# Attention with a key and value cache: every score product as a pair of 64-row tiles, the third dimension block crossing to the other bank, and new instruction lists

## The chip, the cores and the metric

The kernel runs on one core of one Trainium2 chip. The core has a matrix engine (TensorE, in the profile PE for its matmuls and PEld for its weight loads), VectorE (DVE), ScalarE (ACT), GpSimd (POOL) and SyncE (SP), which here only issues transfers. Each engine works through its own list of instructions; engines wait for each other through semaphores. The metric is the time of one execution on the device in microseconds, the median of several runs. The profile is of one execution.

## The reference: what is computed

```python
B, Sq, D = 8, 112, 640
H, Sk, Dh = 32, 512, 192
q = (x @ wq).reshape(B, Sq, H, Dh).transpose(0, 2, 1, 3)
scores = einsum("bhqd,bhkd->bhqk", q, k_cache) * Dh ** -0.5
p = softmax(scores, axis=-1)
o = einsum("bhqk,bhkd->bhqd", p, v_cache)
return o.transpose(0, 2, 1, 3).reshape(B, Sq, H * Dh) @ wo
```

All inputs are bf16. Eight batches, 32 heads, 112 query rows, 512 keys and a head size of 192, which is one and a half times the 128 rows of the matrix array. That odd size is what the change is about.

## The kernel before

The heads are taken in four rounds of eight. A *step* `n` (64 of them) is one batch and four heads of a round (`place`, L74); a *group* `g` (eight of them) is a round and half of the batches. For each group, `q_fill` (L584) projects the queries of two heads at a time: a pair of heads has 384 dimensions, so three blocks `c` of 128 dimensions, each five matmuls that write a PSUM bank, which `evQ` on ScalarE copies to the SBUF tile `qr`. For each step, in order of its own data:

- `qc` (L608, VectorE) copies `qr` to the tile `qh` with the two halves of 64 partitions exchanged, so that either half of a dimension block is to be had in either half of the partitions.
- `scores` (L618, TensorE) multiplies queries by keys. The keys stand transposed in `kt`. A column of `kt` holds two neighbouring keys, an even and an odd one, whose 2 x 192 dimensions lie one after another over three blocks of 128 rows: block 0 and the first half of block 1 belong to the even key, the second half of block 1 and block 2 to the odd one. A head has 256 such columns. Scores of even keys go to the even bank of a pair `j` of heads (banks 0 and 2), those of odd keys to the odd bank (1 and 3), 256 columns a head. A step has 8 matmuls over 128 rows (`Sm`, L635 and L637: block 0 to the even bank, block 2 to the odd one) and then 8 over 64 rows (`St`, L648 and L650: the halves of block 1, as four pairs that use the upper and the lower half of the array).
- `softmax` (L655): `smax` (VectorE, L663) scales and finds the maximum from PSUM, `exp` (ScalarE, L668), `rc` and `norm` (VectorE, L680 and L672).
- `transposes` (L694) turn the probabilities on TensorE in pairs of 64 and 48 rows (`PT`, L706); `evPT` (L719) copies them out. Five late steps are turned by a transfer instead (`TD`, L690).
- `values` (L722) multiply by the values: `PVt` (L739) in tiles of 64 columns, then `PVm` (L750) in full ones; `evPV` (ScalarE, L760) writes `oT_sb`.
- Per group, `o_half` (L767, L772) multiplies by `wo`, and `oacc` (VectorE) adds over the rounds. `OF` and `oout` turn and store the result.

The keys of the first seven pairs of head sets and batches are transposed on TensorE (`KT`, L561, copied by `evK`, L572); the others come transposed by the transfer itself (L139).

The order of all this is written out by hand: `ORDER_PE`, `ORDER_ACT`, `ORDER_DVE` and `ORDER_SP` list the operations of each engine. `Plan.run` (L35) goes through an engine's list, and before each operation waits for those that it depends on, with a semaphore count per engine. Row-tiled operations count on two semaphores, `PE` and `PE2`, one for each half of the array. A PSUM bank passes from one user to the next by a dependency on the copy that emptied it (`fill`, L896). Three layouts of the array occur: 128 rows by 128 columns (`Q`, `O`, `PVm`, `Sm`), 64 rows (`St`, `PT`, `KT`) and 128 by 64 (`PVt`).

The matmuls of one step's scores, before:

```python
e.matmul(ps[0:SQ, 2 * j, hs], ev, ktb[:, :, 0, cs(i)], start=(h == 0), stop=False, ...)           # Sm, even bank
mm = e.matmul(ps[0:SQ, 2 * j + 1, hs], od, ktb[:, :, 2, cs(i)], start=(h == 0), stop=False, ...)  # Sm, odd bank
m1 = e.matmul(ps[0:SQ, 2 * j, hs], ev, ktb[0:64, :, 1, cs(i)], start=False, stop=True, ...)       # St, rows 0 to 63
m2 = e.matmul(ps[0:SQ, 2 * j + 1, hs], od, ktb[64:128, :, 1, cs(i)], start=False, stop=True, ...) # St, rows 64 to 127
```

Of the kernel before, what the change touches and what calls it, by code (L numbers as in the profile page):

```python
# [11 lines left out]
class Plan:  # L12

# [6 lines left out]
    def add(self, eng, name, deps, emit, sem=None, inc=1):  # L20
        assert name not in self.ops, name
        self.ops[name] = dict(eng=eng, deps=deps, emit=emit, sem=sem or eng, inc=inc)

    def number(self):
        self.count = {}
        for eng, names in self.order.items():
            for n in names:
                o = self.ops[n]
                o["at"] = {}
                for s in o["sem"] if isinstance(o["sem"], tuple) else (o["sem"],):  # L30
                    self.count[s] = self.count.get(s, 0) + o["inc"]
                    o["at"][s] = self.count[s]
        assert sum(map(len, self.order.values())) == len(self.ops)

    def run(self, eng_name, eng, sems):  # L35
        seen = {}
        for n in self.order[eng_name]:
            o = self.ops[n]
            need = {}
            for d in o["deps"]:  # L40
# [12 lines left out]
def build_mha_kernel(nc, x, k_cache, v_cache, wq, wo, out):  # L53
# [9 lines left out]
    NP = NN // 2  # L63
# [3 lines left out]
    KS, VS, QS = 4, 3, 2 * LP  # L67
    NPL = 7
# [17 lines left out]
    with ExitStack() as es:  # L86
# [9 lines left out]
        qr = sb("qr", [128, QS, 3, SG], BF16)  # L96
        qh = sb("qh", [128, 2, 2, 4, SQ], BF16)
# [21 lines left out]
        q_flat = qr[:].rearrange("p l c s -> p (l c s)")  # L119
        late = [wq_flat[:, i * 16 * SQ:(i + 1) * 16 * SQ] for i in range(4)] + [q_flat[:, 0:16 * SQ]]  # L120
# [10 lines left out]


        def load_k(i):
            r, b = divmod(i, B)
            name = ("K", i)
# [4 lines left out]
            deps = [("St", 2 * (i - KS) + 1, 3)] if i >= KS else []  # L140
            if i == KS - 1:
                deps = [("XT", c) for c in range(4)]
            add("SP", name, deps, emit, f"mK{i % KS}", 16)

        def load_v(i):
# [5 lines left out]
            deps = [("PVm", 2 * (i - VS) + j, 1) for j in range(2)] if i >= VS else []  # L151
# [26 lines left out]
        def load_wq(r, lp, n):  # L178
# [6 lines left out]
            add("SP", ("WQ", r, lp, n), [("Q", 2 * r - 1, lp + i, c) for i in range(n) for c in range(3)] if r else [],  # L185
# [3 lines left out]
        def load_wo(r):  # L189
# [6 lines left out]

        ORDER_PE = [
# [7 lines left out]
            ("K", 2, 3, 0, "DVE", "DVE"), ("K", 1, 0, 4, "DVE", "ACT"), ("K", 1, 1, 2, "ACT", "DVE"),  # L205
# [5 lines left out]
            ("K", 3, 2, 4, "ACT", "DVE"), ("PVm", 2), ("S", 6), ("K", 4, 1, 4, "ACT", "DVE"),  # L211
            ("K", 4, 2, 6, "ACT", "DVE"), ("K", 4, 0, 4, "ACT", "DVE"), ("K", 4, 3, 0, "ACT", "DVE"),
# [3 lines left out]
            ("Q", 2, 2, 1, 4), ("K", 5, 2, 6, "ACT", "DVE"), ("S", 9), ("PVt", 5, 4), ("PVm", 5),  # L216
            ("K", 6, 2, 6, "ACT", "DVE"), ("PT", 7, 0), ("Q", 2, 2, 2, 6), ("Q", 2, 1, 1, 7), ("S", 10),
            ("PVt", 6, 6), ("PVm", 6), ("K", 6, 0, 4, "ACT", "DVE"), ("K", 6, 3, 0, "ACT", "DVE"), ("PT", 8, 6),
            ("Q", 2, 3, 1, 1), ("Q", 2, 2, 0, 0), ("PVt", 7, 5), ("PVm", 7), ("Q", 2, 3, 0, 1),
            ("K", 6, 1, 4, "ACT", "DVE"), ("PT", 9, 6), ("S", 11), ("PVt", 8, 4), ("PVt", 9, 6), ("PVm", 9),  # L220
# [317 lines left out]
        for kind, *a in ORDER_PE:  # L538
            size = {"PVt": 1, "PT": 1, "O": 3, "O6": 2, "OF": 1}.get(kind)
            if size and len(a) > size:  # L540
                bank_of[(kind, *a[:size])] = a[size]
# [498 lines left out]
```

## Time and profile before

| what | value |
|---|---|
| median of three runs | 444.96 us (444.37 to 445.19) |
| span of the profiled execution | 444.4 us |
| TensorE matmuls | 6805, busy 425.1 us |
| VectorE busy | 363.2 us |
| ScalarE busy | 344.4 us |
| moved by transfers | 122.02 MB, 275 GB/s |

The span runs from the first to the last instruction of the profiled execution; the median is of other executions and has in it what lies around the span. Matmuls are pipelined: the next starts before the last has ended, so the distance between two starts is what a matmul costs TensorE, and the duration of one is longer. In a timeline a row gives the start, the duration, the engine, the line of the kernel, the operation and its operands with their shapes: `64*112 64x256` is 64 rows of the array, 112 columns of weights, 256 moving columns. A group's row gives count, busy time, mean, and the idle time ahead of it with what ended it.

### The profile page before, as it was taken

The page shows a single profiled execution, that of the slowest core. Times are in us where ns is not written, and L with a number is a line of the kernel's source. Part 1 is how long each engine was busy: PE and PEld are TensorE (multiplying, and loading weights), DVE is VectorE, ACT ScalarE, POOL GpSimd, SP SyncE. Part 2 cuts the span into 40 slices and gives each one's busy share as a digit, 9 for nine tenths or more (in the row PEclk, how much of TensorE's full clock was granted, in tenths as well). Part 3 has the DMA queues.
Part 4 walks back from the last instruction along what each step waited for, and adds up shares of the span by engine and source line. Part 5 has one row for each costly group of instructions (what it writes and reads, how often), then busy time and mean ns, then how long its engine had stood idle before and what let it go on. Part 6 is the DMA issues. An engine that isn't in the chain of part 4 may idle for free.

```text
span 444.4 us, 16108 instructions
## 1 busy us (share of the span) xinstructions
PE 425.1 (96%) x6805; PEld 304.5 (69%) x6805; DVE 363.2 (82%) x1165; ACT 344.4 (78%) x770; POOL 0.7 (0%) x6
## 2 busy tenths in 40 slices
PE   6998989889999999999899999999999999899995
PEld 4666666666677667777677766767667766676895
DVE  1579999879699889888989798889799888969871
ACT  3699999887678687978869688788778758965773
POOL 0000000000000000000000000000000000000000
PEclk9999999999999999999999999999999999989999
DMA  8999999998999999999999999999999999999952
GB/s 278 373 337 323 347 299 285 226 342 276 232 289 317 215 270 270 365 247 288 238 223 324 301 236 267 360 370 234 234 266 313 256 267 371 234 173 242 237 176 80
DMA packets 222184, 122.02 MB, mean 275 GB/s; under 512 B 164640, under 2 KB 222112, under 8 KB 222112
## 3 DMA queue, kind: packets, MB, share of 16 engines
q1 hardware_dynamic: 222112, 120.99, 106.6%
q8 instruction: 54, 0.88, 0.8%
q14 instruction: 18, 0.15, 0.1%
HBM read 78.22 MB, written 1.15 MB: 179 GB/s over the span
## 4 chain that ended last, share of the span: by engine, by line
PE 84%; DVE 5%; ACT 5%; DMA 4%; issue 2%; SPq 0%; ACTq 0%
PE ps L772 19%; PE ps L590 18%; PE ps L750 12%; PE ps L648 7%; PE ps L739 7%; PE ps L635 6%; PE ps L637 6%; PE ps L706 5%; DVE s_sb L663 3%; DMA wo_sb<-in_k_cache_dram 2%; PE ps L561 2%; ACT p_sb L668 2%; DMA wq_sb<-in_wq_dram 2%; ACT qr L595 1%; DVE p_sb L672 1%
## 5 line engine op out<-in xcount | busy, mean ns | idle before, releaser
L668 ACT ACTIVATE p_sb<-s_sb,nmx 112x512 bf16<-112x512 f32 x256 | 182.8, 717 | 31.6 <-DVE s_sb L663 26.8
L663 DVE TENSOR_SCALAR_CACHE_REDUCE s_sb<-ps 112x512 f32<-112x512 f32 x256 | 169.4, 684 | 29.6 <-PE ps L650 20.8
L590 PE MATMUL ps<-xT_sb,wq_sb 128*128 128x448 bf16 x480 | 102.0, 353 | 3.3 <-DMA wq_sb<-in_wq_dram 2.3
L772 PE MATMUL ps<-oT_sb,wo_sb 128*128 128x448 bf16 (+1 forms) x480 | 93.3, 341 | 0.1
L672 DVE TENSOR_SCALAR p_sb<-p_sb,rinv 112x512 bf16<-112x512 bf16 x256 | 81.3, 347 | 1.5
L590 PEld LDWEIGHTS ps<-xT_sb,wq_sb 128*128 128x128 bf16 x480 | 42.9, 98 | 41.5 <-DMA wq_sb<-in_wq_dram 2.9
L772 PEld LDWEIGHTS ps<-oT_sb,wo_sb 128*128 128x128 bf16 x480 | 44.3, 98 | 35.0 <-DVE pT_sb L719 0.5
L760 ACT ACTIVATE oT_sb<-ps 128x672 bf16<-128x672 f32 x64 | 46.3, 726 | 25.8 <-PE ps L750 25.4
L595 ACT ACTIVATE qr<-ps 128x448 bf16<-128x448 f32 x96 | 49.6, 539 | 12.7 <-PE ps L590 12.1
L750 PE MATMUL ps<-pT_sb,vt 128*128 128x112 bf16 x944 | 55.8, 215 | 2.0 <-issue 2.0
L719 ACT ACTIVATE pT_sb<-ps 128x768 bf16<-128x768 bf16 x59 | 47.0, 801 | 12.8 <-PE ps L706 12.8
L750 PEld LDWEIGHTS ps<-pT_sb,vt 128*128 128x128 bf16 x944 | 48.1, 99 | 6.3 <-issue 2.1
L668 ACT ACTIVATION_READ_ACCUMULATOR p_sb<-s_sb,nmx 112x1 f32 x256 | 49.5, 193 | 0.0
L719 DVE COPY pT_sb<-ps 128x1024 bf16<-128x1024 bf16 x59 | 40.3, 683 | 3.4 <-PE ps L706 2.6
L706 PE MATMUL ps<-ident,p_sb 64*128 64x64 bf16 (+1 forms) x1888 | 37.3, 185 | 1.2 <-issue 0.6
L706 PEld LDWEIGHTS ps<-ident,p_sb 64*128 64x128 bf16 (+1 forms) x1888 | 33.3, 94 | 5.8 <-DVE p_sb L672 2.0
L635 PE MATMUL ps<-kt,qr 128*112 128x256 bf16 x128 | 36.0, 282 | 0.9 <-ACT oT_sb L760 0.4
L637 PE MATMUL ps<-kt,qh 128*112 128x256 bf16 x128 | 35.2, 275 | 1.1 <-issue 1.1
L635 PE MATMUL ps<-kt,qh 128*112 128x256 bf16 x128 | 35.1, 274 | 0.0
L637 PE MATMUL ps<-kt,qr 128*112 128x256 bf16 x128 | 35.0, 274 | 0.0
L650 PE MATMUL ps<-kt,qh 64*112 64x256 bf16 x128 | 34.1, 291 | 0.1
L648 PE MATMUL ps<-kt,qr 64*112 64x256 bf16 x128 | 34.0, 291 | 0.0
(62 smaller groups left out, 478.6 us busy)
## 6 DMA issues: line engine op xcount, KB each, us to landing
vt<-in_v_cache_dram SPq DMA_DIRECT2D x32, 1536.0 KB, 9.0
wo_sb<-in_wo_dram SPq DMA_DIRECT2D x4, 1920.0 KB, 12.7
wq_sb<-in_wq_dram SPq DMA_DIRECT2D x14, 480.0 KB, 5.7
wo_sb<-in_k_cache_dram SPq DMA_DIRECT2D x3, 1536.0 KB, 9.3
accT<-in_k_cache_dram SPq DMA_DIRECT2D x3, 1536.0 KB, 12.7
vt<-in_k_cache_dram SPq DMA_DIRECT2D x2, 768.0 KB, 10.0
out_dram<-xT_sb SPq DMA_DIRECT2D x8, 140.0 KB, 3.2
wq_sb<-in_wq_dram SPq DMA_DIRECT2D x1, 960.0 KB, 10.6
```

The costliest lines, as they stand in the source:

```text
L590: mm = e.matmul(ps[:, bank, 0:SG], wq_sb[:, dc, c0:c0 + 128], xT_sb[:, dc, bh * SG:(bh + 1) * SG], start=(dc == 0), stop=(dc == DC - 1))
L595: return e.activation(qr[:, q_slot(g, lp), c, :], ps[:, bank, 0:SG], ACTF.Copy)
L635: e.matmul(ps[0:SQ, 2 * j, hs], ev, ktb[:, :, 0, cs(i)], start=(h == 0), stop=False, skip_group_check=True)
L637: mm = e.matmul(ps[0:SQ, 2 * j + 1, hs], od, ktb[:, :, 2, cs(i)], start=(h == 0), stop=False, skip_group_check=True)
L648: m1 = e.matmul(ps[0:SQ, 2 * j, hs], ev, ktb[0:64, :, 1, cs(i)], start=False, stop=True, skip_group_check=True)
L663: return e.tensor_scalar(s_sb[:, a, :].rearrange("p (e c) -> p e c", e=2), ps[0:SQ, 2 * j:2 * j + 2, h * 256:(h + 1) * 256], -scale, None, ...
L668: return e.activation(p_sb[:, k, :], s_sb[:, a, :], ACTF.Exp, bias=nmx[:, k:k + 1], scale=-1.0, accum_out=rsum[:, k:k + 1])
L672: return e.tensor_scalar(p_sb[:, k, :], p_sb[:, k, :], rinv[:, k:k + 1], None, op0=ALU.mult)
L706: ends.append(e.transpose(psb[:, bank + t, i * w:(i + 1) * w], p_sb[lo:hi, (4 * n + k) % 8, q * 128:(q + 1) * 128], ident[lo:hi, lo:hi]))
L719: return e.activation(dst, src, ACTF.Copy) if j == 0 else e.tensor_copy(dst, src)
L750: mm = e.matmul(ps[:, b0 + j, 2 * h * SQ:(2 * h + 1) * SQ], vtb[:, h0 + 2 * j + h, d0:d0 + 128], pT(j, h, q), start=(q == 0), stop=(q == 3))
L772: mm = e.matmul(ps[:, bank_of["O", g, m, 0], 0:nc_], wo_sb[:, k, m * 128:(m + 1) * 128], oT_sb[:, g % 2, k, 0:nc_], start=(k == 0), stop=( ...
```

## The change

The scores of a step are now 24 matmuls over 64 rows, all in pairs, one in the upper and one in the lower half of the array. Each of the three 128-row blocks of the keys is taken as two halves. `straight` (`S1`, one for each pair `j` of heads) has the halves that the array's own half suits: rows 0 to 63 of blocks 0 and 1 to the even bank, rows 64 to 127 of blocks 1 and 2 to the odd bank, four pairs. `swapped` (`S2`) has what is left: rows 0 to 63 of block 2 to the odd bank, rows 64 to 127 of block 0 to the even bank, two pairs. Since the halves then change banks, `S2` of a `j` depends on `S1` of the same `j`, which is a wait of TensorE for its own two semaphores. In the lists `S1` of both `j`, then `S2` of both `j` always stand together.

The query weights have 128 columns in place of 112: 16 columns of whatever stands behind them are read with them and give 16 rows of scores that nobody reads. `qr` and `qh` get 16 columns of padding, which VectorE fills with zeros at the start, together with the never written slots of `qh` (four memsets; TensorE waits for them before its list).

All lists are new: the order on TensorE, ScalarE, VectorE and SP, and a table `BANKS` that gives each operation its bank. The operations other than the scores are the same and as many; three key copies and one copy of `x` go from ScalarE to VectorE. The machinery of the banks is written anew (`tiles` in place of `fill`); places for paired projections (`QPAIRS`) and for a GpSimd list are there and empty.

```diff
-        qr = sb("qr", [128, QS, 3, SG], BF16)
-        qh = sb("qh", [128, 2, 2, 4, SQ], BF16)
+        qr = sb("qr", [128, QS * QP], BF16)
+        qh = sb("qh", [128, 2 * 2 * 4 * SQ + 16], BF16)
...
+        def q_at(n, j, c, lo, hi):
+            r, b, qd = place(n)
+            c0 = (q_slot(group(n), 2 * qd) + j) * QP + c * SG + b % (B // 2) * SQ
+            return qr[lo:hi, c0:c0 + 128]
+
+        def h_at(n, j, k, lo, hi):
+            c0 = ((n % 2 * 2 + j) * 4 + k) * SQ
+            return qh[lo:hi, c0:c0 + 128]
...
+            def mm(e, j, h, odd, q, blk, lo, first, last):
+                hs = slice(h * 256, (h + 1) * 256)
+                return e.matmul(ps[:, 2 * j + odd, hs], q, ktb[lo:lo + 64, :, blk, cs(2 * j + h)],
+                                start=first, stop=last, skip_group_check=True)
+
             for j in range(2):
-                def emit(e, j=j):
+                def straight(e, j=j):
                     for h in range(2):
...
+                        f = h == 0
+                        if h == 0:
+                            ev = [q_at(n, j, 0, 0, 64), q_at(n, j, 1, 0, 64)]
+                            od = [h_at(n, j, 0, 64, 128), h_at(n, j, 1, 64, 128)]
+                        else:
+                            ev = [h_at(n, j, 2, 0, 64), h_at(n, j, 3, 0, 64)]
+                            od = [q_at(n, j, 1, 64, 128), q_at(n, j, 2, 64, 128)]
+                        for i in range(2):
+                            a = mm(e, j, h, 0, ev[i], i, 0, f and i == 0, False)
+                            b = mm(e, j, h, 1, od[i], 1 + i, 64, f and i == 0, False)
+                    return a, b
+
+                def swapped(e, j=j):
+                    for h in range(2):
+                        od, ev = ((h_at(n, j, 1, 0, 64), q_at(n, j, 0, 64, 128)) if h == 0 else
+                                  (q_at(n, j, 2, 0, 64), h_at(n, j, 2, 64, 128)))
+                        a = mm(e, j, h, 1, od, 2, 0, False, True)
+                        b = mm(e, j, h, 0, ev, 0, 64, False, True)
+                    return a, b
+                keys = ([("evK", n // 2, 2 * qd + j, t) for t in range(2)] if n // 2 < NPL else [("K", n // 2)])
+                add("PE", ("S1", n, j), [("qc", n)] + keys, straight, ("PE", "PE2"))
+                add("PE", ("S2", n, j), [("S1", n, j)], swapped, ("PE", "PE2"))
...
-                add("DVE", ("smax", n, i), [("St", n, 2 * j + 1), ("exp", *old)], smax)
+                add("DVE", ("smax", n, i), [("S2", n, j), ("exp", *old)], smax)
...
+            e.memset(qr[:].rearrange("p (l w) -> p l w", w=QP)[:, :, 3 * SG:QP], 0.0)
+            e.memset(qh[0:64, 0:16 * SQ].rearrange("p (j k s) -> p j k s", j=4, k=4)[:, :, 0, :], 0.0)
+            e.memset(qh[64:128, 0:16 * SQ].rearrange("p (j k s) -> p j k s", j=4, k=4)[:, :, 3, :], 0.0)
+            e.memset(qh[:, 16 * SQ:], 0.0).then_inc(zINIT, 1)
```

A stretch of TensorE's list around step 27, before and after (`S` stands for all of a step's scores; the last number of an entry before is its bank):

```diff
-            ("PT", 24, 6), ("O", 2, 0, 0, 4), ("O", 2, 0, 1, 4), ("S", 27), ("PT", 25, 4), ("O", 2, 1, 0, 7),
-            ("O", 2, 1, 1, 7), ("Q", 4, 2, 2, 4), ("Q", 4, 2, 0, 0), ("PVt", 24, 5), ("PVm", 24), ("S", 28),
...
+            ('PVm', 23, 1), ('PT', 24), ('Q', 4, 2, 0), ('O', 1, 3, 0), ('O', 1, 3, 1), ('PT', 25), ('S1', 27, 0),
+            ('S1', 27, 1), ('S2', 27, 0), ('S2', 27, 1), ('PVt', 24), ('Q', 4, 3, 1), ('PVm', 24, 0), ('PVm', 24, 1),
```

More of the change, by code (lines that the diff above doesn't have):

```diff
@@ L39, in run @@
             need = {}
-            for d in o["deps"]:
+            for d in o["deps"] + o["banks"]:
                 if d in self.ops:
@@ L67, in build_mha_kernel @@
     KS, VS, QS = 4, 3, 2 * LP
+    QP = 3 * SG + 16
     NPL = 7
@@ L118, in build_mha_kernel @@
         wq_flat = wq_sb[:].rearrange("p a b -> p (a b)")
[L119 to L120 removed]
+        late = [wq_flat[:, i * 16 * SQ:(i + 1) * 16 * SQ] for i in range(4)] + [qr[:, 0:16 * SQ]]
         pT_late = dict(zip(BY_DMA, late))
@@ L535, in build_mha_kernel, with x_transposes @@
             add("SP", ("OUT", b), [("oout", b)], emit, f"mOUT{b % DC}", 16)
-        bank_of = {}
[L538 to L541, printed above, removed]
-        def x_transposes(c, bank, eng):
+        bank_of = {tuple(t): b for t, b in BANKS}
+        def x_transposes(c):
+            bank = bank_of["XT", c]
             def emit(e):
@@ L831, in emit @@
                 return mm
-            add("PE", ("OL", s, part), [("evPV", NN - 2 + s)], emit)
+            add("PE", ("OL", s, part), [("evPV", NN - 2 + i) for i in range(s + 1)] + [("WO", NR - 1)], emit)
         def o_last_acc(part):
@@ L844, in emit @@
                 return mm
-            add("DVE", ("oaccL", part), [("OL", 1, part)], emit)
+            add("DVE", ("oaccL", part), [("OL", 1, part)] + [("oacc", NG - 3, m) for m in range(DC)], emit)
         def o_final(b):
@@ L959, in build_mha_kernel @@
+        order["PE"], order["ACT"], order["DVE"] = ORDER_PE, ORDER_ACT, ORDER_DVE
+        order["POOL"], order["SP"] = ORDER_POOL, ORDER_SP
+        holder = {}
+        for op in ORDER_PE:
+            for bank, evacs in tiles(op):
+                P.ops[op]["banks"] = P.ops[op]["banks"] + holder.get(bank, [])
+                holder[bank] = evacs
         P.number()
@@ L998, in _ @@
                             pattern=[[-1, 128]], channel_multiplier=1).then_inc(gINIT, 1)
+            P.run("POOL", e, sems)
     return nc
```

762 lines of the change are left out of this document (365 added, 397 removed), and 203 rows, old and new, of tables (BANKS, ORDER_PE, ORDER_SP).

## The prediction

> **What bounds the kernel now.** I read the page first: busy time, then the chain that ended last.
>
> ```profile
> span 444.4 us, 16108 instructions
> PE 425.1 (96%) x6805; PEld 304.5 (69%) x6805; DVE 363.2 (82%) x1165; ACT 344.4 (78%) x770; POOL 0.7 (0%) x6
> q8 instruction: 54, 0.88, 0.8%
> PE 84%; DVE 5%; ACT 5%; DMA 4%; issue 2%; SPq 0%; ACTq 0%
> ```
>
> TensorE is busy for 96% of the span and holds 84% of the chain; VectorE and ScalarE have a fifth to spare. The table by stretches says where TensorE is not the bound (columns: stretch, its length, busy time and count of PE, PEld, DVE, ACT, POOL, granted clock, DMA share, GB/s).
>
> ```profile
> 40.00:60.00 20.00, 17.24 (x397) 13.46 (x397) 18.18 (x60) 18.17 (x42) 0.00 (x0) 1.00 0.95 320
> 60.00:80.00 20.00, 18.80 (x428) 13.47 (x425) 19.58 (x61) 19.95 (x43) 0.00 (x0) 1.00 1.22 311
> 80.00:100.00 20.00, 17.25 (x380) 12.67 (x378) 15.32 (x49) 16.84 (x36) 0.00 (x0) 1.00 1.06 286
> 100.00:140.00 40.00, 39.89 (x591) 28.12 (x589) 34.42 (x113) 29.59 (x70) 0.00 (x0) 1.00 1.10 268
> 390.00:394.00 4.00, 4.00 (x57) 3.66 (x53) 0.44 (x2) 2.34 (x6) 0.00 (x0) 0.62 1.27 288
> 430.00:445.00 15.00, 9.55 (x240) 8.96 (x236) 4.03 (x12) 5.57 (x8) 0.00 (x0) 0.97 0.20 60
> ```
> ```profile
> 160.00:200.00 40.00, 40.00 (x621) 28.28 (x620) 35.42 (x117) 33.97 (x79) 0.00 (x0) 1.00 1.15 292
> ```
>
> From 40 to 100 us TensorE idles 6.7 us (2.8 + 1.2 + 2.8), while keys and weights still arrive; in the middle it hardly idles, so there a nanosecond less of TensorE work is a nanosecond less of time, as long as the other engines keep up. What it does per step is read from the timeline of one score block (start, duration, one matmul a line; the odd-bank partner of each 64-row pair is left out).
>
> ```profile
> 203.93 0.28 PE L635 MATMUL ps<-kt,qr 128*112 128x256 bf16 x1
> ...
> 204.70 0.27 PE L637 MATMUL ps<-kt,qr 128*112 128x256 bf16 x1
> 204.90 0.31 PE L648 MATMUL ps<-kt,qr 64*112 64x256 bf16 x1
> ...
> 205.06 0.27 PE L648 MATMUL ps<-kt,qh 64*112 64x256 bf16 x1
> ...
> 205.27 0.27 PE L648 MATMUL ps<-kt,qh 64*112 64x256 bf16 x1
> ...
> 205.38 0.63 PE L706 MATMUL ps<-ident,p_sb 64*128 64x64 bf16 x32
> ```
>
> Starts count here, not durations, since matmuls overlap. Eight 128-row matmuls start 0.110 us apart (203.93 to 204.70 in seven steps); the last is followed after 0.20, not 0.11; the second pair comes 0.16 after the first; from there pairs come 0.107 apart (205.06 to 205.38 in three). A pair costs what one matmul of 128 rows costs, because its halves run side by side. So the block has 0.09 us of changing from 128 to 64 rows, 0.05 of a first pair whose weights were not loaded ahead, and 1.31 of streaming: 1.45 in all, 64 times.
>
> **The change, part by part.**
>
> *Streaming.* Sixteen matmuls (eight full, four pairs) become 24 in twelve pairs. Before 8 x 0.110 + 4 x 0.107 = 1.31 us, after 12 x 0.107 = 1.28: -0.024 x 64 = **-1.5 us**. That a pair over crossed banks keeps 0.107 is taken from the pairs of before, which also write an even and an odd bank.
>
> *Changes of the array's layout.* The inner one goes, but a block that follows 128-row work now has one at its entry. That any change costs about the same shows in the chain: ten query matmuls followed by their own kind of layout take 1.89 us, followed by 64-column tiles 2.00.
>
> ```profile
> 104.03 1.89 PE ps L590 x10
> 105.92 0.19 PE ps L772
> ```
> ```profile
> 174.85 2.00 PE ps L590 x10
> 176.85 0.52 PE ps L739 x16
> ```
>
> So 0.09 to 0.11; I take 0.10. Neighbours in the two TensorE lists, counted: before 254 changes (89 into 64 rows, 64 of them inside score blocks; 112 into 128x128; 53 into 128x64), after 226 (79, 93, 54). Score blocks entered from 64-row work are 30 where there were 5, left into 64-row work 30 where there were 45. 28 x 0.10 = **-2.8 us**.
>
> *The first weights after a change.* These rows give min/median/max of each operation's duration; the excess of max over the steady value is the part of the load that shows.
>
> ```profile
> L648 PEld LDWEIGHTS ps<-kt,qr x128: 122/125/127, 18.5 to 424.1; 64*112 64x112 bf16 x128
> L648 PE MATMUL ps<-kt,qr x128: 269/291/313, 18.5 to 424.2; 64*112 64x256 bf16 x128
> ```
> ```profile
> L706 PEld LDWEIGHTS ps<-ident,p_sb x1888: 92/94/97, 36.1 to 431.5; 64*128 64x128 bf16 x102, 48*128 48x128 bf16 x87
> L706 PE MATMUL ps<-ident,p_sb x1888: 179/189/200, 36.2 to 431.5; 64*128 64x64 bf16 x102, 48*128 48x48 bf16 x87
> ```
>
> With 112 columns 313 - 269 = 44 ns show, with 128 columns 200 - 189 = 11. Before 64 x 0.044 = 2.8 us; after 34 entries with a change x 0.011 = 0.4: **-2.4 us**. The low end of this term is none (if 128 columns load as slowly here: 34 x 0.044, so -1.3), the high end -2.8. The rows of 128 columns are transposes. The Trainium skill, "TensorE: Matmul & The Clock Gate", section "Weight-path perf modes", says that a fast load is on whenever the weights are 128 columns and not fp32, which would make them the same for score products; no run here shows that yet.
>
> *The new wait.* The two swapped pairs of bank pair j wait for the straight ones of the same j, on both semaphores (S2 on S1). S2 of j=0 has the four straight pairs of j=1 in front of it, 0.43 us, and is covered. S2 of j=1 has two pairs, 0.21, in front. Behind it on TensorE's queue stands everything, and VectorE's maxima wait for S2. The trace has no wait of TensorE on itself; the nearest row is a wake by VectorE.
>
> ```profile
> 85.27 0.08 DVE L663 DVE_READ_ACCUMULATOR s_sb<-ps 112x1 f32 x1
> 85.41 0.13 PEld L635 LDWEIGHTS ps<-kt,qr 128*112 128x112 bf16 x1 [0.23 <-DVE s_sb L663]
> 85.41 0.32 PE L635 MATMUL ps<-kt,qr 128*112 128x256 bf16 x1
> ```
>
> The accumulator read ends at 85.35, the load starts at 85.41: 0.06 us. A straight pair ends 0.27 after its start, so S2 can start at 0.33, where it would have come at 3 x 0.107 = 0.32; its weights then were not loaded ahead (+0.011). That is 0.02; I take 0.03, x 64 = **+1.9 us**. Ends: 0 (the signal comes in time) and 0.12 (a second 0.06 because two semaphores are waited for one after the other, and 0.044 of load): 0 to +7.7 us.
>
> *More instructions.* 512 more matmuls, 512 more loads and 128 more stand-alone waits: 1,152 on 13,610. Four or five times TensorE stood with nothing that the profile shows to wait for.
>
> ```profile
> PEld ps L561 <- issue: 3.5, 6, 1.2
> ...
> PEld ps L750 <- issue: 2.1, 1, 2.1
> ...
> PEld ps L637 <- issue: 1.3, 1, 1.3
> ```
>
> That is 6.9 us, and after the longest the clock fell to 0.62 for four microseconds (the stretch from 390), 1.5 us more. I read these as instructions arriving late (54 packets of them on the page), and scale: 6.9 x 1152 / 13610 = **+0.6 us**. Ends: all gone, -8.4; two more like the longest, +5.
>
> *Lists, banks, set-up.* The lists hold the same transposes, projections, value and output products, and SP's the same 100 transfers in another order; POOL's list is empty. Four evacuations go from ScalarE to VectorE, both off the path. SP mostly waits for buffers, so its transfers start when TensorE frees them:
>
> ```profile
> SPq L139 <- PE ps L706: 80.1, 8, 14.6
> ```
> ```profile
> DVE xT_sb L553 <- PE ps L546: 5.4, 2, 4.1
> ```
>
> Four memsets are put ahead of VectorE's list; VectorE idles 4.1 us there, so nothing; with that cover gone, four small operations, and the accumulator read above takes 0.08: some 0.3 us. The order itself I cost at 0, for want of a row: it can give back at most the 6.7 us of 40 to 100, and can cost as much as the other engines fall behind.
>
> *Sum.* -1.5 - 2.8 - 2.4 + 1.9 + 0.6 = -4.2 us on the span of 444.4: 440.2. The runs' median lies 0.6 above the span (444.96), so 440.8; I say **440.8 us**. About 0.2% is what a measurement here can tell from no change.
>
> **Rivals.**
>
> 1. *The wait decides (slower).* Without it the sum is -6.1 us, so it eats all at 6.1 / 64 = 0.095 us a step. For: two semaphores, S2's weights behind the wait. Against: the wake of 0.06 in the row above. At 0.12 it costs 7.7: 440.8 + 5.8 = 446.6. Chance 0.15.
> 2. *The new order leaves TensorE idle (slower).* In the middle there is no idle to lose and 18 to 22% of slack on the others; but VectorE already waits for the score products, and a block whose probabilities are transposed earlier waits for the softmax. At 0.15 us a step, 9.6: 450.4. Against: transposes still stand about two steps behind their scores in both lists. Chance 0.14.
> 3. *The early stage gains too.* Half of the 6.7 us of 40 to 100 goes: 437.4. Against: bytes arrive at 286 to 320 GB/s there whatever the order. Chance 0.12.
> 4. *It doesn't do what it says.* Crossed pairs run one after the other, four a step: 4 x 0.107 x 64 = 27: 468. Against: the even/odd pairs of before. Chance 0.02.
> 5. *Weight loads show in every pair.* Eight more pairs a step, each with 0.011 to 0.044 us of load: +5.6 to +22.5, so 446 to 463. Against: pairs 0.107 apart while their loads take 0.125 in the same rows. Chance 0.02. The Trainium skill, same page, "What overlaps and what doesn't", says that loads overlap running matmuls only in other row groups, which would be this rival; the 0.107 speaks against it, the measurement decides.
> 6. *No change that counts.* Gains and wait cancel. Chance 0.07.
>
> **How the numbers follow.** The forecast has the remaining 0.48. Faster by over 0.2%: it and rival 3, 0.60; same 0.07; slower, 1, 2, 4 and 5, 0.33. The forecast's own range, with the wait from 0 to 0.06 and the loads' ends, is 438 to 444. For eight in ten I reach from 436 (rival 3 with the late instructions partly gone) to 449 (rival 1 and most of rival 2).
>
> **What would show it.** In the changed kernel's timeline: twelve pair starts a block, 0.107 apart, with a gap only before the last two; no gap inside otherwise; an entry gap of 0.09 in about 34 blocks; weight loads of about 95 ns, not 125. The row of 64 waits "issue" ahead of the 64-row load goes; a row of 64 TensorE waits on TensorE comes, and its size is the price of S2. Wrong would be: that gap at 0.1 or more, TensorE idle in stretches from 100 to 380, or chosen stretches with more idle than 40 to 100 has now.

## The result and the profile after

The changed kernel takes 456.28 us (median of five executions, 454.65 to 462.82), the kernel before 444.37 on the same chip (442.32 to 445.19): a ratio of 1.0259, 95% interval 1.0217 to 1.0301. Forecast were 440.8 us and 436 to 449. Executions more than 1.5% above the shortest of their kernel are left out of every ratio of this document (here two, of 462.52 and 462.82 us; most of all in the kernel before shifted by 128 places, below, six of ten). The profiled execution is the one of 462.52 (span 460.7), so its stalls are more than those of the median. Sums below go by the ratios, with 1% as 4.45 us.

The page of the changed kernel, the lines that answer those of before:

```profile
span 460.7 us, 17282 instructions
PE 430.9 (94%) x7317; PEld 290.3 (63%) x7317; DVE 367.0 (80%) x1173; ACT 343.8 (75%) x766; POOL 0.7 (0%) x6
q8 instruction: 58, 0.95, 0.8%
PE 71%; DVE 5%; DMA 5%; issue 4%; ACT 2%; DVEq 0%; ACTq 0%
```

TensorE's share falls from 96 to 94% and "issue" on the chain rises from 2 to 4%. The table by stretches says that the loss is no longer early alone (columns as before: stretch, length, busy time of PE, PEld, DVE, ACT, POOL, granted clock, DMA share, GB/s):

```profile
40.00:60.00 20.00, 16.87 (x378) 11.95 (x377) 17.79 (x58) 17.51 (x37) 0.00 (x0) 0.91 0.82 283
60.00:80.00 20.00, 16.39 (x303) 10.43 (x304) 13.86 (x43) 13.96 (x32) 0.00 (x0) 0.91 0.77 217
80.00:100.00 20.00, 18.87 (x410) 13.10 (x409) 18.13 (x59) 18.53 (x43) 0.00 (x0) 1.00 1.12 288
100.00:140.00 40.00, 38.18 (x688) 25.97 (x684) 35.13 (x112) 32.22 (x71) 0.00 (x0) 1.00 1.18 268
160.00:200.00 40.00, 39.58 (x664) 26.42 (x662) 34.97 (x113) 32.02 (x76) 0.00 (x0) 1.00 1.20 250
220.00:260.00 40.00, 37.62 (x609) 24.83 (x609) 30.81 (x100) 29.13 (x65) 0.00 (x0) 1.00 1.15 254
```

The last of these stretches in the kernel before:

```profile
220.00:260.00 40.00, 38.80 (x597) 27.69 (x595) 34.29 (x113) 31.07 (x73) 0.00 (x0) 1.00 1.17 267
```

From 100 to 140 us TensorE idles 1.8 us where it idled 0.1 before, from 220 to 260 2.4 us where it idled 1.2, and from 40 to 80 the granted clock is 0.91 where it was 1.00. What ended the idle time is in the table of TensorE's waits (us in total, times, longest):

```profile
PEld ps L744 <- PE ps L744: 13.0, 61, 0.2
PEld ps L857 <- issue: 8.0, 22, 1.8
PEld ps L688 <- issue: 6.7, 15, 3.6
PEld ps L891 <- issue: 5.3, 13, 2.7
PEld ps L744 <- issue: 5.2, 12, 1.2
PEld ps L825 <- issue: 5.2, 7, 1.9
PEld ps L744 <- DVE s_sb L781: 4.7, 13, 0.7
PEld ps L640 <- issue: 3.8, 5, 2.0
```

Two things are new: the wait of score products for score products, 61 times 0.21 us, and "issue" rows with single stalls of up to 3.6 us ahead of every kind of work. Before, the longest was 2.1 us, and the three rows with the long ones came to 6.9 us. The wait in the timeline of one block, its last pairs and the value products behind it (one matmul or two a line):

```profile
293.71 0.27 PE L744 MATMUL ps<-kt,qh 64*128 64x256 bf16 x1
...
293.82 0.32 PE L744 MATMUL ps<-kt,qh 64*128 64x256 bf16 x2
293.93 0.27 PE L744 MATMUL ps<-kt,qr 64*128 64x256 bf16 x1
294.16 0.27 PE L744 MATMUL ps<-kt,qh 64*128 64x256 bf16 x1
...
294.48 0.58 PE L857 MATMUL ps<-pT_sb,vt 128*64 128x112 bf16 x16
```
```profile
294.13 0.09 PEld L744 LDWEIGHTS ps<-kt,qh 64*128 64x128 bf16 x1 [0.22 <-PE ps L744]
```

Pairs start 0.11 apart up to 293.93, the next only 0.23 later. The last straight pair starts at 293.71 and ends at 293.98; the load that waits for it starts at 294.13, 0.15 us after that end. Over the blocks that lie in one piece in the trace, the median from this pair to the next is 0.234 in place of 0.109: 0.125 us a step, 64 x 0.125 = 8.0 us.

The longest of the other stalls (TensorE's rows alone):

```profile
62.12 0.13 PEld L688 LDWEIGHTS ps<-xT_sb,wq_sb 128*128 128x128 bf16 x2 [3.56 <-issue]
62.12 2.42 PE L688 MATMUL ps<-xT_sb,wq_sb 128*128 128x448 bf16 x6 [3.12 <-issue]
```

The profile shows nothing that this matmul waits for; the six matmuls then take 2.42 us, some 0.4 each, where ten took 1.89 before, and from 62.1 to 65.4 us the granted clock is 0.50. The trace has TensorE's instructions arriving in 58 packets (54 before) of 16 KB; 58 x 256 is 14,848, and TensorE executes 14,916 instructions with its separate waits, so a packet holds 256. Counting TensorE's instructions up to the end of packet number n, it never gets further than 256 n + 193 before that packet has landed, in any of the twenty traces of this study. At the stall above it stands at exactly 193 for the whole 1.1 us of the transfer, then goes on 1.4 us after the packet's end. So stalls like this one are **instructions that come late**: TensorE has used up what it holds. Packets that landed with at most eight instructions left were 3 before and 7 after.

### The profile page after: what moved, and what is told of

It is laid out like the page before. It is cut to its first block, busy times and chain, and to the rows that moved or that the text cites. A ratio compares the mean times of both kernels' runs of the same rounds, so it can differ in the third digit from the quotient of the medians.

```text
span 460.7 us, 17282 instructions
## 1 busy us (share of the span) xinstructions
PE 430.9 (94%) x7317; PEld 290.3 (63%) x7317; DVE 367.0 (80%) x1173; ACT 343.8 (75%) x766; POOL 0.7 (0%) x6
## 4 chain that ended last, share of the span: by engine, by line
PE 71%; DVE 5%; DMA 5%; issue 4%; ACT 2%; DVEq 0%; ACTq 0%
PE ps L744 17%; PE ps L891 16%; PE ps L688 15%; PE ps L869 10%; PE ps L857 6%; PE ps L825 6%; DVE s_sb L781 2%; DMA wo_sb<-in_wo_dram 2%; DMA wq_sb<-p_sb 1%; ACT p_sb L786 1%; DMA qr<-p_sb 1%; PE ps L640 1%; DVE p_sb L790 1%; PE ps L924 1%; PE ps L948 1%
## 5 line engine op out<-in xcount | busy, mean ns | idle before, releaser
L744 PE MATMUL ps<-kt,qh 64*128 64x256 bf16 x768 | 106.3, 271 | 1.1 <-issue 1.1
L744 PE MATMUL ps<-kt,qr 64*128 64x256 bf16 x768 | 104.7, 272 | 1.4 <-DVE s_sb L781 0.6
L891 PE MATMUL ps<-oT_sb,wo_sb 128*128 128x448 bf16 (+1 forms) x480 | 95.1, 346 | 3.6 <-DMA wo_sb<-in_wo_dram 2.6
L744 PEld LDWEIGHTS ps<-kt,qh 64*128 64x128 bf16 x768 | 62.7, 95 | 18.8 <-PE ps L744 13.0
L744 PEld LDWEIGHTS ps<-kt,qr 64*128 64x128 bf16 x768 | 59.4, 94 | 13.4 <-DVE s_sb L781 4.7
L133 ACT ACTIVATE qr<-ps 128x448 bf16<-128x448 f32 x96 | 50.9, 539 | 20.5 <-PE ps L688 19.6
L133 ACT ACTIVATE pT_sb<-ps 128x768 bf16<-128x768 bf16 x59 | 47.2, 802 | 15.7 <-PE ps L825 15.0
L857 PE MATMUL ps<-pT_sb,vt 128*64 128x112 bf16 x944 | 33.8, 217 | 3.6 <-issue 2.7
L857 PEld LDWEIGHTS ps<-pT_sb,vt 128*64 128x64 bf16 x944 | 25.9, 110 | 14.7 <-issue 7.0
## 6 DMA issues: line engine op xcount, KB each, us to landing
wo_sb<-in_wo_dram SPq DMA_DIRECT2D x4, 1920.0 KB, 10.9
```

What stands on the lines that cost most here:

```text
L133: return e.activation(dst, src, ACTF.Copy)
L744: return e.matmul(ps[:, 2 * j + odd, hs], q, ktb[lo:lo + 64, :, blk, cs(2 * j + h)], start=first, stop=last, skip_group_check=True)
L857: mm = e.matmul(ps[64 * h:64 * h + 64, b0 + j, SQ:2 * SQ], vtb[:, h0 + 2 * j + h, d0:d0 + 64], pT(j, h, q), start=(q == 0), stop=(q == 3))
L891: mm = e.matmul(ps[:, bank_of["O", g, m], 0:nc_], wo_sb[:, k, m * 128:(m + 1) * 128], oT_sb[:, g % 2, k, 0:nc_], start=(k == 0), stop=(k = ...
```

## The experiments

Theories: **W**, the wait is the loss; **L**, a wait on its own work takes from TensorE the lead with which its instructions come in; **N**, the new lists cost the rest; later **F**, packets of instructions stand behind data transfers; **A**, the place where packets end decides; **D**, their density does. All ratios are to the kernel before on the same chip, with the 95% interval.

### Which part of the change loses: products, wait, lists

*Four pairs ahead of each wait* (`e1_cover`): for `j = 0` the swapped pairs come first.

```diff
+                parts = (swapped, straight) if j == 0 else (straight, swapped)
-                add("PE", ("S1", n, j), [("qc", n)] + keys, straight, ("PE", "PE2"))
-                add("PE", ("S2", n, j), [("S1", n, j)], swapped, ("PE", "PE2"))
+                add("PE", ("S1", n, j), [("qc", n)] + keys, parts[0], ("PE", "PE2"))
+                add("PE", ("S2", n, j), [("S1", n, j)], parts[1], ("PE", "PE2"))
```

> For the first pair of heads (j = 0) the two swapped pairs now come first and the four straight ones second; for j = 1 it stays as it is. Lists, products and waits are as many as in the changed kernel, the scores are the same, but each S2 now has four pairs, 0.43 us, between it and the S1 it waits for. Theory W (the wait itself): the gap of 0.125 us a step goes, 64 x 0.125 = 8.0 us, so about 448 from 456. Theory L (a wait on its own work also takes from TensorE the lead with which its instructions come in, so that late instructions show): the wait is still there, so the longer 'issue' stalls, 18 us in the changed kernel against 7 before, stay; also about 448. Theory N (the new lists cost the rest): also about 448. If the gap is no matter of how much work lies in between, no change: 456.

*No crossing, no wait* (`e2_uncross`):

```diff
-                        a = mm(e, j, h, 1, od, 2, 0, False, True)
-                        b = mm(e, j, h, 0, ev, 0, 64, False, True)
+                        a = mm(e, j, h, 0, od, 2, 0, False, True)
+                        b = mm(e, j, h, 1, ev, 0, 64, False, True)
...
-                add("PE", ("S2", n, j), [("S1", n, j)], swapped, ("PE", "PE2"))
+                add("PE", ("S2", n, j), [], swapped, ("PE", "PE2"))
```

> The swapped pairs add to the bank of their own array half and don't depend on the straight ones: the same 24 matmuls, weights and lists as in the changed kernel, no wait of TensorE on itself. It changes the result: the second half of block 0 and the first half of block 2 go to the other key's scores. W: the 8.0 us go, 448. L: the 8.0 us go and the 'issue' stalls fall from about 18 to about 7 us, 456 - 8 - 11 = 437, as forecast for the change without a wait (438.9). N: 448, with the stalls as long as in the changed kernel.

*Old products in the new lists* (`e3_oldprod_newlists`), with the matmuls of `Sm` under the name `S1` and of `St` under `S2`:

```diff
-                add("PE", ("S1", n, j), [("qc", n)] + keys, straight, ("PE", "PE2"))
-                add("PE", ("S2", n, j), [("S1", n, j)], swapped, ("PE", "PE2"))
+                add("PE", ("S1", n, j), [("qc", n)] + keys, full)
+                add("PE", ("S2", n, j), [], halves, ("PE", "PE2"))
```

> The new lists, banks and set-up, with the old products: S1 is the four matmuls over 128 rows of a pair of heads, S2 the two 64-row pairs, 112 columns of weights, no wait of TensorE on itself. W and L: the lists cost nothing, about 444 (and 6 fewer changes of layout into the block than in the old lists' place: within 2 us of it). N: the lists bring the rest, so 444 + 7 = 451 or more, with idle time of TensorE in the stretches from 100 to 380 us.

*New products in the old lists* (`e4_newprod_oldlists`): the lists and the banks of before, with `("S", n)` written out:

```diff
-            ("S", 0),
+            ('S1', 0, 0), ('S1', 0, 1), ('S2', 0, 0), ('S2', 0, 1),
...
```

> The new products with their wait in the old lists and banks. The old lists have 254 changes of layout less the 64 inside the blocks plus those at their entries (59 blocks come after other layouts): 249 or so, so 0.5 us gained there in place of 2.8. W: 444.4 - 1.5 - 0.5 - 2 + 8 = 448. L: 448 plus the longer stalls, about 456 to 459. N: 448, the rest of the loss gone with the new lists.

| kernel | median us | ratio |
|---|---|---|
| four pairs ahead of each wait | 458.07 | 1.0245 (1.0173 to 1.0318) |
| no crossing, no wait | 450.47 | 1.0105 (1.0067 to 1.0143) |
| old products, new lists | 455.23 | 1.0214 (1.0172 to 1.0257) |
| new products, old lists | 461.93 | 1.0354 (1.0312 to 1.0395) |

All three theories asked for 448 from the covered wait; it is as slow as the changed kernel. Without the wait the time falls by 1.54%, 6.9 us, and stays slower than before: W holds for its own share only. L falls: it asked for 437, and 4 packets still land at the last moment without the wait (3 before); the wait's price also proves the same without the transfers (below). That the lists cost something (N) seems so from 1.0214, but the new products lose more in the old lists than in the new ones (461.93, where 448 or 456 to 459 was expected), so it isn't the lists alone. The covered wait shows where its 8 us went:

```profile
PEld ps L744 <- DVE s_sb L783: 10.6, 27, 1.1
...
PEld ps L744 <- PE ps L744: 1.4, 2, 0.8
```

The wait on TensorE's own work is gone (13.0 to 1.4 us), but the second pair of heads starts two pairs earlier, and waits for the maxima of the step before (4.7 to 10.6 us): its banks are not empty yet. Splitting the products by head, which would put enough pairs ahead of each wait without starting a bank early, wasn't tried: both halves of the array would then write one bank at the same time, without a wait between them.

### Late instructions and the data transfers

Four kernels, and later three more, each with 54 of the 100 transfers left out, so that little else moves from 100 us on:

```diff
-            ("V", 3),
...
-            ("K", 7), ("K", 8),
...
-            ("K", 31),
...
-            ("V", 31),
```

> The kernel before, with the value loads after the third and the transposed key loads after the seventh left out (54 of the 100 transfers): later steps compute with the keys and values that are in the tiles already, so the result is another one; TensorE, VectorE and ScalarE do the same work. Theory F (packets of TensorE's instructions stand behind data transfers and come late): the stalls without a releaser, 7 us in the trace of before, and part of the waits for transfers go, so about 436. Theory I (the stalls come from the order and the other engines): no change beyond the 2 to 4 us of waits for transfers, 442 or more.

> The changed kernel with the same loads left out. F: no late instructions, so what is left over the kernel before without its loads is the sum of the direct terms: 28 changes of layout fewer (-2.8), first weights (-2.4), streaming (+0.6, pairs 0.109 apart as in the trace), wait (+8.0): +3.4 us. I: the difference stays as it is with the loads, +11 or 12 us.

> The products without crossing and without the wait, new lists, the same loads left out. F: 8.0 us less than the changed kernel without its loads, so 4 to 5 us less than the kernel before without its loads; that would be the forecast without its wait. I: as with the loads, 4 us more than the kernel before without its loads.

> The old products in the new lists, the same loads left out. F: 33 changes of layout more than in the old lists (287 against 254 by the trace), so +3.3 us over the kernel before without its loads. I: +9 us, as with the loads (455.2 against 446.1).

| kernel, loads left out | median us | ratio | over the kernel before without loads |
|---|---|---|---|
| before | 438.9 | 0.9851 (0.9814 to 0.9887) | |
| changed | 442.92 | 0.9927 (0.9904 to 0.9950) | +0.76%, 3.4 us |
| no crossing, no wait | 435.92 | 0.9785 (0.9753 to 0.9817) | -0.66%, 2.9 us |
| old products, new lists | 441.94 | 0.9911 (0.9883 to 0.9939) | +0.60%, 2.7 us |

F foresaw +3.4, -4 to -5 and +3.3 us; theory I +11, +4 and +9. F is the nearer by far: without the transfers the direct terms are nearly all that is left, and the 11.5 us of the changed kernel shrink to 3.4. That this is F's figure to the tenth is luck: the wait costs less than the 8.0 in it, and the gains are smaller (below). For the kernel before F said about 436 and I 442 or more; 438.9 lies between. The stretches of the changed kernel without loads show it (columns as above):

```profile
100.00:140.00 40.00, 40.00 (x723) 27.45 (x722) 36.77 (x119) 33.12 (x76) 0.00 (x0) 1.00 0.04 9
220.00:260.00 40.00, 39.98 (x677) 26.97 (x677) 35.90 (x118) 32.56 (x76) 0.00 (x0) 1.00 0.01 2
340.00:380.00 40.00, 40.00 (x641) 25.53 (x636) 36.97 (x120) 31.76 (x75) 0.00 (x0) 1.00 0.01 3
```

At 2 to 9 GB/s in place of some 260, TensorE idles no more, with the same matmuls in the same order: 1.8 and 2.4 us of idle time became 0.00 and 0.02. Its waits:

```profile
PEld ps L739 <- PE ps L739: 13.5, 63, 0.2
PEld ps L852 <- issue: 5.9, 21, 0.9
```

The wait on itself is untouched by the transfers (13.5 us against 13.0), so the difference of 0.9927 and 0.9785, 6.3 us, is its price by itself. It is less than the 8.0 us of gaps: without the wait TensorE waits longer for VectorE, 7.0 us for the probabilities and 5.3 for the maxima in place of 5.3 and 4.3, which gives part of the gain back. In the kernel before without its loads "issue" has only short stalls left, beside the 64 at the inner change of layout:

```profile
PEld ps L643 <- issue: 11.4, 64, 0.2
PEld ps L734 <- issue: 4.0, 17, 0.4
...
PEld ps L701 <- DVE p_sb L667: 2.3, 8, 0.5
...
PEld ps L556 <- issue: 1.1, 3, 0.4
```

From the place 110 instructions ahead of a multiple of 256, a packet's end comes on average 5.7 us later in the kernel before and 6.0 in the changed one, with all loads, and 3.4 us later in both without (40 to 440 us): the transfers delay a packet by 2.3 to 2.6 us. What TensorE consumes in that time differs: 256 of its instructions last 8.4 us on average with the old products and 7.7 with the new ones (100 to 400 us, without loads), and 17% of all such runs of 256 last under 7 us in the kernel before, 33% in the changed one.

Leaving out the transfers takes more away than late instructions, since TensorE also waits for the data. Ahead of matmuls, "issue" gaps are 5.6 us in the kernel before and 14.2 in the changed one, and 0.0 and 4.3 without the loads; gaps that a transfer ends are 3.7 and 5.2 us, and 3.3 and 0.5 without. The same matmuls are busy for 430.9 us in the changed kernel and 426.7 without the loads, after fewer stretches at a lower clock. So late instructions, late data and the clock each have a part in what the changed kernel loses more; that the profiled execution is a long one makes their sizes rough.

*The covered wait without loads* (`f5_cover_noload`):

> The order with four pairs ahead of each wait, with the same loads left out as in the others. Theory W (what the wait costs is the gap behind it, and here the gap is gone): the 7.0 us by which the crossed products lay above the uncrossed ones without loads go, 436. Theory B (the second pair of heads starts two pairs earlier, and VectorE has not emptied its banks yet: the waits of the score products for the maxima were 10.6 us in the trace with loads, 4.7 in the changed kernel): only 1 to 2 us go, 441.

441.25 us, ratio 0.9933 (0.9904 to 0.9962): by the ratio the same as the changed kernel without loads, by the medians 1.7 us less. B: the wait for the maxima (11.1 us, 4.3 in the changed kernel without loads) took the place of the wait for itself.

### Is it luck where the packets end?

The instructions are shifted by 64, 128 or 192 places through more, smaller idle matmuls and fulfilled waits ahead of the work; the first real matmul starts 0.1 to 0.5 us later, the first projection between 0.5 earlier and 0.5 later.

```diff
-                mm = e.matmul(ps[:, 5, 0:256], zeros[:, 0:128], zeros, start=True, stop=True)
+                mm = e.matmul(ps[:, 5, 0:92], zeros[:, 0:128], zeros[:, 0:92], start=True, stop=True)
+                for _ in range(64 * (i + 1) // n - 64 * i // n):
+                    e.wait_ge(zINIT, 1)
...
-            idle(e, 18)
+            idle(e, 50)
```

> The kernel before, with 64 waits that are long fulfilled among the 18 idle matmuls at the very start, so that every later TensorE instruction lies 64 places further on in the packets of 256. All else is the same. Theory A (whether a packet comes too late is a matter of which dense stretch its end falls on): the late packets, 6 of 54 before, fall elsewhere; the time moves by 2 to 10 us from 446. Theory D (it is the number of instructions per microsecond alone): within 1 us of 446, but for what the waits cost at the start, at most 1 us.

> The kernel before, shifted by 128 places: 50 idle matmuls of 92 columns in place of 18 of 256 (64 more instructions, the same columns in all) and 64 fulfilled waits among them. A: the time moves by 2 to 10 us, another way than with 64. D: within 1 us of 446, but for up to 2 us at the start.

> The changed kernel, shifted by 128 places in the same way. A: the time moves by several us from 457, up or down; if the place of the packets was the kernel's bad luck, down to 450. D: 457 as it was, 10 late packets or so.

> The kernel before, shifted by 192 places (82 idle matmuls of 56 columns, 64 fulfilled waits). Theory A alone (the changed kernel lost by the place of its packets, not by their number): over the four places the kernel before and the changed kernel spread over the same extra time, 4 us apart by the direct terms; the mean of the kernel before, so far 449.4 over the places 0, 64 and 128, would come near 453. Theory A with D (place and number): its mean stays near 449, within 444 to 453 here.

> The changed kernel, shifted by 64 places. A alone: its mean over the places, 460.4 over 0 and 128 so far, comes down to the kernel before's plus 4, so 448 to 452 here. A with D: 456 to 464.

> The changed kernel, shifted by 192 places. A alone: 448 to 452. A with D: 456 to 464.

| places | before | changed |
|---|---|---|
| 0 | 1 | 1.0259 (1.0217 to 1.0301) |
| 64 | 1.0125 (1.0049 to 1.0201) | 1.0288 (1.0213 to 1.0363) |
| 128 | 1.0047 (0.9995 to 1.0100) | 1.0455 (1.0380 to 1.0531) |
| 192 | 1.0069 (1.0036 to 1.0103) | 1.0344 (1.0253 to 1.0435) |

The place matters: 5.6 us at most for the kernel before, 8.7 for the changed one, with the same work. In the changed kernel shifted by 128 places the stalls are as long as they get:

```profile
PEld ps L746 <- PE ps L746: 13.4, 63, 0.2
PEld ps L746 <- issue: 8.2, 10, 4.1
PEld ps L827 <- issue: 8.2, 10, 2.1
PEld ps L893 <- issue: 6.6, 13, 4.0
```

At 128 places the kernel before is less steady than its row says: its ten executions run from 444.43 to 455.73 us, and their median of 452.44 is 1.0174 of the 444.72 at place 0. In its profiled execution (455.15 us) six packets land with at most eight instructions left, where there were 3.

But luck isn't the cause: both kernels stand at the best of their four places as they are, the means are 1.0060 and 1.0337, 12.3 us apart (10.9 with the 1.0174), and no place brings the changed kernel to the kernel before at its worst. "A alone" falls. The last three (447.54, 459.23 and 462.75 us) lie where A with D had them: the loss belongs to the kernel and not to the place. Whether it comes with the number of instructions, these runs can't tell, since the lists differ too.

### Products or lists, and the one part that costs nothing

> The new products with their wait in the old lists, the same loads left out. Direct terms against the kernel before without its loads (438.9): 10 changes of layout fewer (244 against 254 in the trace, -1.0), first weights (-1.5, as just measured), streaming (+0.6), wait (+7.0): 444. If so, the loads cost 18 us here (461.9 with them) against 13 for the old products in the new lists: the products, not the lists, bring most of it. If the new lists bring it, the time here lies near 454.

444.88 us, 0.9986 (0.9958 to 1.0014): as expected from the direct terms, within 1 us.

The query weights of 128 columns alone, with the old products and lists (made from the kernel with old products in new lists, so with the new bank machinery and memsets), with and without the loads:

```diff
-                return e.matmul(ps[0:SQ, 2 * j + odd, hs], q[:, 0:SQ], ktb[lo:hi, :, blk, cs(2 * j + h)],
+                return e.matmul(ps[:, 2 * j + odd, hs], q, ktb[lo:hi, :, blk, cs(2 * j + h)],
```

> The old products in the old lists with query weights of 128 columns in place of 112, and the loads left out as before; this prices the first weights after a change by themselves. By the forecast's term: 64 x 0.033 us less than the kernel before without its loads, 438.9 - 2.1 = 436.8. If 128 columns load no faster here: 438.9.

> The old products in the old lists with query weights of 128 columns and all loads: the one part of the change that gains without more instructions or waits. 444.8 - 1.5 = 443.3, with some 4 us either way for where the packets fall.

Without loads 437.4 us, 0.9815 (0.9746 to 0.9884), 1.6 us less than the kernel before without them, whose 0.9851 lies inside that interval, so the times alone don't show a gain; in the trace the second pair of a block follows the first after 0.12 us in place of 0.15 (medians, 0.034 less), 2.2 us over 64 steps. The rows of this kernel have every matmul within 16 ns of the shortest, where the kernel before had 44:

```profile
L765 PEld LDWEIGHTS ps<-kt,qr x512: 92/96/98, 19.1 to 416.4; 128*128 128x128 bf16 x86, 64*128 64x128 bf16 x85
L765 PE MATMUL ps<-kt,qr x512: 267/272/283, 19.1 to 416.5; 128*128 128x256 bf16 x86, 64*128 64x256 bf16 x85
```

With the loads 444.3 us, 0.9989 (0.9951 to 1.0027): no change that can be told from none, so no kernel of this study that has all its loads is shown to be faster than the one before. What the loads cost each kernel, as the difference of its two ratios:

| products, lists | packets | cost of the loads |
|---|---|---|
| old, old | 54 | 1.49%, 6.6 us |
| old with 128 columns, old | 53 | 1.74%, 7.7 us |
| old, new | 53 | 3.03%, 13.5 us |
| uncrossed, new | 58 | 3.20%, 14.2 us |
| covered wait, new | 58 | 3.12%, 13.9 us |
| changed, new | 58 | 3.32%, 14.8 us |
| changed, old | 58 | 3.68%, 16.4 us |

These are uncertain by 2 to 4 us each. Either the new products or the new lists take the cost from 7 to 14 us or so, and both together to no more. For the products this fits D (more packets, denser runs of instructions), and the traces of the new products in the old lists bear it out: with the loads, "issue" gaps ahead of matmuls are 14.0 us in place of 4.7, gaps that a transfer ends 1.8 in place of 1.6, and busy time is 434.8 in place of 426.9 us at a granted clock of 0.985 in place of 1.000.

For the new lists with the old products D doesn't fit: their runs are no denser (12% of 256 instructions in under 7 us) and their trace has 2 packets at the last moment. Its "issue" gaps are 3.4 us, none without the loads, and its longest gap is a wait for values that are still on their way:

```profile
PE ps L851 <- DMA vt<-in_v_cache_dram: 2.6, 1, 2.6
```

But that trace is of the shortest of five executions (451.18 us; the others took 455.04 to 455.46), so how the lists lose the rest stays open.

## Why the prediction was wrong

A gain of 4.2 us was forecast and a loss of 11.5 measured. Two terms of the sum were mis-sized, the wait (by 4.4 us) and what was counted as more instructions (by 7.5); together they are 12 of the 15.7 us. Two of the prediction's own signs of being wrong came: the gap is over 0.1 us, and TensorE is idle in stretches after 100 us.

- *Streaming, forecast -1.5.* Measured 0: pairs start 0.109 apart in both kernels, by the trace's starts. The 0.107 was worked out from three steps, the last of which ended at a transpose and not at a pair, against 0.110 from seven rounded rows.
- *Layout changes, -2.8.* Right: 226 changes, as counted. The old products in the new lists have 287, 33 more than before, for 2.7 us without loads, so 0.08 each if the lists cost nothing else; the inner change adds 0.094 us to the distance of two starts (0.203 in place of 0.109, medians). So 28 fewer are -2.3 to -2.6 us.
- *First weights, -2.4.* Right by the starts: before, the second pair of 64 blocks came 0.044 us late, 2.8 us; in the changed kernel it comes 0.010 late in 35 of 61 blocks, 0.4 us. The kernel with 128 columns alone gains 2.2 by the starts (64 x 0.033 = 2.1 was expected) and 1.6 by times that are too uncertain to show it. The rows of the changed kernel confirm the loads: 94 ns where 125 stood.

```profile
L744 PEld LDWEIGHTS ps<-kt,qr x768: 92/94/148, 18.8 to 435.6; 64*128 64x128 bf16 x192
L744 PE MATMUL ps<-kt,qr x768: 266/269/418, 18.8 to 435.7; 64*128 64x256 bf16 x192
```

  The Trainium skill, "TensorE: Matmul & The Clock Gate", "Weight-path perf modes", has the fast load on for 128 columns that aren't fp32; these rows agree.
- *The new wait, +1.9.* **This step failed.** It took the wake of TensorE by VectorE, 0.06 us, and overlap for nearly all of it. TensorE's own signal took 0.15 us from the end of the matmul to the load, and the gap is 0.125 a step in the trace, just past the upper end of 0.12: 8.0 us; by the times it is 6.9 us with loads and 6.3 without. Even that is just over rival 1's measure of 6.1 us, so the wait eats the forecast's gain; but that rival's 446.6 still left 10 us out.
- *More instructions, +0.6.* **This step failed too.** It scaled the stalls by the number of instructions, 8%. The part of the loss that comes with the transfers is 11.5 - 3.4 = 8.1 us, more than the whole of the stalls before. The reading of the stalls as late instructions was right for the long ones. What was missed is that a packet is late or not by a margin. That the new products bring late instructions is shown in the old lists, where waits for data don't grow; that they do it because a denser stream uses the margin up fits the runs of 256 and isn't shown apart. In the changed kernel the 8.1 us also hold late data and the lower clock behind stalls. The range's end of +5 was too near.
- *Lists at 0.* With the loads this failed as well: the old products in the new lists are 9.5 us slower than in the old ones (1.0214), and only 2.7 of that is there without loads. It doesn't add to the 8.1 us, since products and lists together cost no more than either. In the direct terms the lists are +1.0 us by difference, 3.4 - (0 - 2.3 - 1.6 + 6.3), which is less than the errors of these figures. The uncrossed kernel without loads shows some of it, transposes that wait for the softmax, 7.0 us where the kernel before without loads had 2.3 (row above):

```profile
PEld ps L820 <- DVE p_sb L785: 7.0, 18, 0.5
```

  That is rival 2 on a small scale. Rival 3 (the early stage gains) fell: from 40 to 80 us TensorE is busy 33.3 us, 36.0 before.
- *Rivals 4 and 5* fell as argued: pairs 0.109 apart, crossed or not, with weight loads of 94 ns in the same rows. The Trainium skill, "TensorE: Matmul & The Clock Gate", "What overlaps and what doesn't", lets a load overlap running matmuls only in other row groups; here the trace disagrees, as it did before.
- *The rest.* 3.4 us of direct terms and 8.1 that come with the transfers make the 11.5 us of the ratio. The forecast without its wait (-6.1) is found as -2.9 in the uncrossed kernel without loads: less than half of what the sum said, with streaming at 0 and more waiting for VectorE.

## What to carry to other kernels

Before counting a change that makes more and shorter instructions, look at how often the busy engine already stands with "issue" and no releaser: here 8% more instructions, or new lists without any, doubled what the transfers cost (7 to 14 us or so), and a shift of the whole program by 64 instructions can move a kernel by a per cent, so a difference of that size needs more than one placement. Price a wait of TensorE for its own last results by a row of that kind (0.15 us here), not by the signal of another engine (0.06). Four pairs, 0.44 us, between the two hid it here where two did not; but check that the new order doesn't ask for a buffer earlier. Leaving the transfers out of both kernels is a cheap way to separate what a change does by itself from what it does to the supply of instructions and data.

## What the runs showed of the hardware

- TensorE's instructions come in packets of 256. In twenty traces it never ran further than 193 past the multiple of 256 whose packet had not landed, and where it stood there for want of a packet it went on 1.3 to 1.6 us after the packet's end (six times in the changed kernel's trace). A packet took 1.1 us on average; it ended 2.3 to 2.6 us later while the loads ran.
- A wait of TensorE for its own matmuls, on two semaphores: 0.15 us from the last matmul's end to the next weight load.
- After some stalls of about 2 us and more the granted clock fell to 0.50 for 3.4 us, with 448-column matmuls 0.4 us apart in place of 0.19: in the changed kernel after stalls of 1.9 and 3.1 us (0.91 from 40 to 80 us), in the kernel before after 2.0 us. After a stall of 2.2 us in the kernel with the covered wait it did not.
- Weights of 128 columns load in 94 ns where 112 columns take 125, and only some 10 ns of the first load after a change show, not 44 (the first interval of a block is 0.119 us, the others 0.109).
